# The gated layer's first product by seven products of halves, a batch at a time, in an attention and mixing kernel on one core

## The chip, the core and the metric

One core of one Trainium2 chip runs the whole program. The metric is device time in microseconds (us) from the first to the last instruction of an execution, and lower is better. The engines are named as in the profile: PE is TensorE (matmuls), PEld its weight loads, DVE is VectorE, ACT is ScalarE, POOL is GpSimd, SP is SyncE, which issues nearly all DMAs here.

## The reference, cut to what matters

Three layers follow each other. Attention over 4 batches x 8 heads, 576 positions and 64 values per head gives x of 4 x 576 x 512; a mixing layer adds a token mix and a channel mix; a gated layer ends it. The change touches the last one:

```
u  = x + (relu(x^T @ w_tok1) @ w_tok2)^T
x2 = u + relu(u @ w_ch1) @ w_ch2                 # 512 -> 1536 -> 512
h  = relu(x2 @ w_in)                             # 512 -> 1024
hp = h padded by one zero position at each end
conv_out = sum over t in 0..2 of conv_w[t] * hp[:, t:t+576, :]
out = (h * sigmoid(conv_out)) @ w_out            # 1024 -> 512
```

All data are 32-bit floats, and the layers' weights are 64-bit floats in memory.

## The kernel before, in words

Every large product runs in halves: a 32-bit operand is scaled by a power of two and split into a 16-bit high part (ScalarE) and a 16-bit low part (the rest; VectorE or GpSimd), and a product is three matmuls, high x high, high x low and low x high (`mm3`, L277 to L282). A column block of 128 outputs over 512 inputs and 288 positions is thus 4 x 3 = 12 matmuls of 128x128 weights and 288 columns.

Positions are cut into 8 chunks of 288 columns, two per batch (`CH`, `NCH`). The program has three stages that overlap. Attention with the token mix and an early part (5 of 12 blocks) of the channel mix runs until about 320 us. Then the rest of the channel mix (`channel_mix` with parts 1 and 2, 4 and 3 blocks), batch after batch, with `mix_input` and `mix_output` around it. Then the gated layer, chunk after chunk (`gated`, L1464).

No order is written by hand. Each step is a task (`T`, which is `Order.add`) with an engine, an assumed duration, a rank, what it reads and writes, and the PSUM buffers that it holds. `Order.run` (L60) plays them through: at each point it takes, on each engine, the task that can start first, and among those that could start at once the one of least rank. The instructions are then issued in that order, so each engine's order is fixed in the program; waits between engines follow from the data. Ranks of the matmuls are raised by `LATE` (1000) once or more, so that the matmuls of an earlier stage go first.

Weights come in blocks of 128x512 (`weight_set`): a DMA of 64-bit values into one of two staging tiles (`wraw`), an exponent step on ScalarE (L317), two joins on VectorE (L321, L322), a sum of squares (L517), then, once all blocks of a set are there and their common scale is known, the split into halves (L551 on ScalarE, L555 on VectorE). The halves of a block are written over the block before it. The slots are `WT[0..40]`: the first 15 (`NE`) lie in a pool that is open from the start, the next 10 (`NA`) in one that opens when attention's tiles are done, the others in one that opens on the left side when the token mix is done. `LATER` holds the ranks of the weights of the mixing parts 1 and 2.

The gated layer before, for each chunk c:

- The chunk of x2 is read back from memory (`chunk`, L598), its largest magnitude taken (L266) and spread to all partitions by a small 32-bit matmul with the identity (`spread`, L260), and the chunk is split (L591 ScalarE, L594 VectorE).
- For each of 8 column blocks m: `hf` is 12 matmuls into one of four PSUM banks ("w"). `relu` (L1508, ScalarE) moves the result to `hp_t[m]`. Then a 286 or 290 column wide gate: `conv0` (L1512, ScalarE), two taps (`conv`, L1518, VectorE), the sigmoid (L1522, ScalarE), the product (`mul`, L1526, VectorE), the high half (`gh`, L269, ScalarE) and the low half (`gl`, L275, GpSimd).
- For each of 4 output blocks d: `outp` is 24 matmuls over all 8 blocks into a "z" bank; `ocopy` (L1545, ScalarE) moves it out and `store` (L1549) issues a DMA.

Of the kernel before, what the change touches and what calls it, by code (L numbers as in the profile page):

```python
# [143 lines left out]
def fox_moe_kernel(  # L144
# [54 lines left out]
    NE = 15  # L199
    NA = 10  # L200
    NW = 41
# [10 lines left out]
    LATER = (-60.0, 0.0, 20.0)  # L212
    PER = 7.0

# [269 lines left out]
    def weight_set(name, blocks, raws, first, ranks, cranks, factor):  # L484

# [5 lines left out]
        bring = power_of if blocks[0][2][0].dtype == F32 else power_of_root  # L491
        if bring is power_of_root:
            factor *= 4.0
        for k, (kind, m, (src, dims)) in enumerate(blocks):
# [66 lines left out]

    us = {}
# [3 lines left out]
    PB = 2  # L566
    taken_res = [0]

    def parts(r):
        if r not in us:  # L570
            us[r] = [work.tile([128, KD, CH], F16, tag=n, name=n, bufs=2) for n in ("uh", "ul")]
        return us[r]
# [25 lines left out]
    def chunk(src, c, rank, reads, evac, scale, measure):  # L598

        r = chunks[0]  # L600
        chunks[0] += 1
        ku = ("u", counted["u"] % UB)
        counted["u"] += 1
        box = {}

        def load():
            box["u"] = pools["p2a"].tile([128, KD, CH], F32, tag="u", name="u", bufs=UB)
            nc.sync.dma_start(box["u"], src[:, :, c * CH:(c + 1) * CH].rearrange("k p s -> p k s"))

        def piece(k, lo):  # L610
            sl = slice(k, k + 2)
            divide(r, sl, lambda: box["u"][:, sl], scale)[lo]()

        T("SP", 0.4, rank - 6, load, reads=[*reads, ("p2a",)], writes=[ku], moved=2.4)
        measure(ku, box, rank + evac)
        for k in range(0, KD, 2):
            kh, kl = [[split_keys(r, x)[y] for x in (k, k + 1)] for y in range(2)]
            o = opening(r)
            rd = [ku, ("scale", id(scale))]
            T("ACT", 0.77, rank + evac, piece, k, 0, reads=[*rd, *o["reads"]], writes=kh + o.get("writes", []))  # L620
            T("DVE", 0.78, rank + evac, piece, k, 1, reads=[*rd, *kh], writes=kl)
        return r, [x for k in range(KD) for x in split_keys(r, k)]

    def channel_mix(c, part, rank, u_of, p_of, rts, tag, tag2, pe, evac):
# [6 lines left out]
        rpool, rbufs, rcount = rts  # L631
# [8 lines left out]
        def rh(m):  # L640
            t = pools[rpool].tile([128, 2, CH], F16, tag="r", name="r", bufs=rbufs)
            box["r", m] = t
            nc.scalar.activation(out=t[:, 0, :], in_=box["z", m], func=AF.Relu)  # L643

        def rl(m):
            t = box["r", m]
            nc.vector.scalar_tensor_tensor(t[:, 1, :], box["z", m], 0.0, f32(t[:, 0, :]), ALU.max, ALU.subtract)  # L647
# [21 lines left out]
        for k, m in enumerate(ms):  # L669
            kz = turn(tag)  # L670
            kr = ("r", rpool, rcount[0] % rbufs)
            rcount[0] += 1
            for j in range(KD):
                T("PE", MM * 3, rank + pe, m1, m, j, reads=[*ukeys, wkey("ch1", m)],
                  writes=[kz, kr, (*kr, "l")], ring=[kz])
            T("ACT", 0.4, rank + evac, rh, m, reads=[kz], writes=[kr], pools=[rpool], ring=[kz])
            T("DVE", 0.46, rank + evac, rl, m, reads=[kz, kr], writes=[(*kr, "l")], pools=[rpool], ring=[kz])
            rkeys += [kr, (*kr, "l")]
        for d in range(KD):
# [6 lines left out]
            for j, m in enumerate(ms):  # L686
                T("PE", MM * 3, rank + pe + 0.01, m2, d, m, pools=[rpool], ring=[kz],
                  writes=[kz, kd] if j == 0 and p_of is None else [kz],
                  reads=[wkey("ch2", x) for x in (ms if j == 0 else [m])] + rkeys + ([kd] if p_of and j == 0 else []))
            if p_of:  # L690
                T("DVE", 0.46, rank + evac, add, d, reads=[kz, back_key], writes=[kd], ring=[kz])
                continue
# [3 lines left out]
    def mix_input(c, rank):  # L696
# [9 lines left out]
        def load_half(x):  # L706
            if x == 0:
                us[r] = [pools["p2a"].tile([128, KD, CH], F16, tag=n, name=n, bufs=2) for n in ("vh", "vl")]
            nc.sync.dma_start(us[r][x], uhl_d[x, :, :, cols].rearrange("k p s -> p k s"))

        def load_u():
            box["u"] = pools["p2a"].tile([128, KD, CH], F32, tag="u", name="u", bufs=UB)
            nc.sync.dma_start(box["u"], u_d[:, :, cols].rearrange("k p s -> p k s"))

        def load_p():
            box["p"] = pools["p2a"].tile([128, KD, CH], F32, tag="p", name="p", bufs=PB)
# [15 lines left out]
    def mix_output(c, p_of, rank):  # L732
# [4 lines left out]
        T("SP", 0.4, rank, store, reads=[(p_of[1], d) for d in range(KD)], writes=[("x2_d", c)], moved=2.8)  # L737
# [5 lines left out]
    px = [power(f"px{c}") for c in range(NCH)]  # L743
    gs = const.tile([128, NCH, 3], F32, name="gs")
    um = [const.tile([128, GB], F32, name=f"um{b}") for b in range(B)]
    xm = [const.tile([128, 1], F32, name=f"xm{c}") for c in range(NCH)]

    with tc.manual_schedule():
# [3 lines left out]
        open_pool("r1")  # L752
        open_pool("we")
        for i in range(NE):
            WT[i] = pools["we"].tile([128, 512], F32, tag=f"w{i}", name=f"w{i}", bufs=1)
# [617 lines left out]
        rts1 = ("r1", 9, [0])  # L1373
# [16 lines left out]
        def turn_a2():  # L1390
            close_pool("a2")
            open_pool("p2a")
            late("p2a", range(NE, NE + NA))

        def turn_left():
# [8 lines left out]
            open_pool("p2b", 1, "left")  # L1404
            late("p2b", range(NE + NA, NW))
            open_pool("cp", 1, "left")
# [14 lines left out]
        at, first = at, at - 1  # L1421
# [11 lines left out]
        rts2 = ("p2a", 9, [0])  # L1433
# [143 lines left out]
        for c in range(NCH):  # L1577
            gated(c)
# [39 lines left out]
```

## Time and profile before

| | us |
|---|---|
| median of 3 runs | 717.15 |
| lowest and highest | 716.79, 717.42 |
| span of the profiled execution | 718.1 |
| TensorE busy in it | 698.7 |
| VectorE, ScalarE, GpSimd busy in it | 507.4, 428.5, 243.4 |

The rows of the trace are in a section below. A busy share is an average over stages with different limits. Matmuls are pipelined, so the mean duration of one (about 286 ns) is not what it costs; the count in a stretch of time tells that. Neighbouring operations of VectorE and ScalarE overlap by some 80 ns in the records, so the step from one start to the next is less than one's duration. The granted clock of 1.00 is the full 2.4 GHz of TensorE.

### The profile page before, as it was taken

What the parts mean: (1) busy time and instruction counts of PE and PEld (TensorE: products, weight loads), DVE (VectorE), ACT (ScalarE), POOL (GpSimd) and SP (SyncE); (2) the same over time, 40 slices, a digit from 0 to 9 for tenths busy, and PEclk for the clock granted to TensorE, in tenths of its full rate; (3) what the DMA queues carried; (4) which work ended last, traced back from release to release, by engine and by line L of the source; (5) the groups of instructions that cost most, each with busy time, mean ns of one, the idle gap of its engine ahead of it and who ended that gap; (6) DMA issues with size and microseconds to landing.
All of it is one profiled execution on the core that took longest, in us unless ns stands there. A gap on an engine that the chain in (4) does not pass through costs nothing.

```text
span 718.1 us, 16399 instructions
## 1 busy us (share of the span) xinstructions
PE 698.7 (97%) x6417; PEld 561.1 (78%) x6417; DVE 507.4 (71%) x1268; ACT 428.5 (60%) x940; POOL 243.4 (34%) x321
## 2 busy tenths in 40 slices
PE   6999888999999999999999999999999999999998
PEld 5889665878877788888888778778888778778786
DVE  6787878999987779537566857435778866875570
ACT  6987776586666544646574645112177766776671
POOL 2247562748453666240000212103023322322240
PEclk9999887999999999999999999999999999999999
DMA  9445769799995979785455765344211111100101
GB/s 225 141 127 189 193 175 235 120 258 226 248 239 138 199 122 223 189 282 150 144 172 147 250 221 161 99 133 144 66 56 58 51 59 34 51 27 25 34 17 50
DMA packets 153117, 101.98 MB, mean 142 GB/s; under 512 B 90000, under 2 KB 145168, under 8 KB 153040
## 3 DMA queue, kind: packets, MB, share of 16 engines
q1 hardware_dynamic: 152944, 100.79, 54.4%
q8 instruction: 50, 0.82, 0.5%
q14 instruction: 27, 0.22, 0.1%
q10 hardware_dynamic: 96, 0.15, 0.1%
HBM read 57.73 MB, written 23.59 MB: 113 GB/s over the span
## 4 chain that ended last, share of the span: by engine, by line
PE 87%; DVE 8%; ACT 1%; DMA 1%; SPq 1%; issue 1%; POOL 0%; DVEq 0%; ACTq 0%
PE w L280 15%; PE w L281 15%; PE w L282 15%; PE z L281 8%; PE z L282 8%; PE z L280 8%; PE z L994 6%; PE w L1083 3%; DVE pl L1033 2%; PE w L1051 2%; PE w L1235 2%; PE z L998 1%; PE w L260 1%; DVE ul L594 1%; PE w L1088 1%; PE w L1089 1%
## 5 line engine op out<-in xcount | busy, mean ns | idle before, releaser
L282 PEld LDWEIGHTS <-w 128*128 128x128 f16 x1280 | 125.6, 98 | 34.0 <-issue 1.9
L280 PEld LDWEIGHTS <-w 128*128 128x128 f16 x1280 | 125.3, 98 | 33.7 <-issue 2.4
L281 PEld LDWEIGHTS <-w 128*128 128x128 f16 x1280 | 125.3, 98 | 33.0 <-issue 1.7
L281 PE MATMUL w<-ul,w 128*128 128x288 f16 x416 | 120.0, 288 | 1.6 <-DVE ul L594 1.6
L280 PE MATMUL w<-uh,w 128*128 128x288 f16 x416 | 120.0, 289 | 1.3 <-ACT uh L591 1.1
L282 PE MATMUL w<-uh,w 128*128 128x288 f16 x416 | 119.9, 288 | 0.0
L275 POOL TENSOR_TENSOR g<-sg,g 128x286 f16<-128x286 f32 (+1 forms) x64 | 55.1, 867 | 150.8 <-ACT g L269 148.0
L1518 DVE SCALAR_TENSOR_TENSOR cv<-hp,cw,cv 128x286 f32<-128x286 f32 (+1 forms) x128 | 75.0, 593 | 38.3 <-ACT cv L1512 36.0
L1018 ACT ACTIVATE t<-t,m 128x192 f32<-128x192 f32 (+4 forms) x160 | 82.0, 551 | 18.1 <-DVE m L1012 14.9
L643 ACT ACTIVATE r<-w 128x288 f16<-128x288 f32 x96 | 39.3, 409 | 88.0 <-PE w L282 87.1
L1012 DVE CUSTOM_DVE_ANT_0 t<-z,mask 128x192 f32<-128x192 f32 (+4 forms) x160 | 70.3, 479 | 12.8 <-PE z L998 12.5
L720 POOL TENSOR_TENSOR p<-p,u 128x288 f32<-128x288 f32 x32 | 26.6, 863 | 149.7 <-DMA p<-p_d 115.1
L647 DVE SCALAR_TENSOR_TENSOR r<-w,r 128x288 f16<-128x288 f32 x96 | 43.3, 453 | 46.8 <-ACT r L643 46.2
L281 PE MATMUL z<-g,w 128*128 128x286 f16 (+1 forms) x256 | 73.3, 286 | 0.0
L280 PE MATMUL z<-g,w 128*128 128x286 f16 (+1 forms) x256 | 73.0, 285 | 0.0
L282 PE MATMUL z<-g,w 128*128 128x286 f16 (+1 forms) x256 | 72.9, 285 | 0.0
L280 PE MATMUL w<-vh,w 128*128 128x288 f16 x224 | 64.1, 286 | 0.0
L281 PE MATMUL w<-vl,w 128*128 128x288 f16 x224 | 64.1, 286 | 0.0
L282 PE MATMUL w<-vh,w 128*128 128x288 f16 x224 | 64.1, 286 | 0.0
L280 PE MATMUL z<-r,w 128*128 128x288 f16 x224 | 64.1, 286 | 0.0
L281 PE MATMUL z<-r,w 128*128 128x288 f16 x224 | 64.1, 286 | 0.0
L282 PE MATMUL z<-r,w 128*128 128x288 f16 x224 | 64.1, 286 | 0.0
(201 smaller groups left out, 1686.8 us busy)
## 6 DMA issues: line engine op xcount, KB each, us to landing
wraw<-in_moe_w_ch_dram SPq DMA_DIRECT2D x24, 512.0 KB, 4.2
qk<-in_qk_dram SPq DMA_DIRECT2D x15, 608.0 KB, 5.4
u_d<-us SPq DMA_DIRECT2D x8, 576.0 KB, 3.4
p_d<-res SPq DMA_DIRECT2D x32, 144.0 KB, 3.1
p<-p_d SPq DMA_DIRECT2D x8, 576.0 KB, 5.3
u<-u_d SPq DMA_DIRECT2D x8, 576.0 KB, 4.8
x_d<-p SPq DMA_DIRECT2D x8, 576.0 KB, 3.2
u<-x_d SPq DMA_DIRECT2D x8, 576.0 KB, 3.9
```

The lines of the kernel that those rows point to most:

```text
L275: nc.gpsimd.tensor_tensor(o, a, b, ALU.subtract)
L280: nc.tensor.matmul(ps, wh, xh, start=(first and i == 0), stop=False)
L281: nc.tensor.matmul(ps, wh, xl, start=False, stop=False)
L282: nc.tensor.matmul(ps, wl, xh, start=False, stop=(last and i == n - 1))
L643: nc.scalar.activation(out=t[:, 0, :], in_=box["z", m], func=AF.Relu)
L647: nc.vector.scalar_tensor_tensor(t[:, 1, :], box["z", m], 0.0, f32(t[:, 0, :]), ALU.max, ALU.subtract)
L720: nc.gpsimd.tensor_tensor(box["p"][:, d], box["p"][:, d], box["u"][:, d], ALU.add)
L994: nc.tensor.matmul(out_[x], t[r, Q0[i]:Q0[i] + 128], t[r, k0:k0 + n], start=first, stop=False)
L1012: nc.vector.tensor_tensor_reduce(to, z_t.pop((n, i)), mk, -0.125, 3e38, ALU.add, ALU.min, m_t[n][0:rows, i:i + 1])
L1018: nc.scalar.activation(out=tt[0:rows, o:o + w], in_=tt[0:rows, o:o + w], func=AF.Exp, bias=m_t[n][0:rows, i:i + 1], scale=-1.0)
L1083: nc.tensor.matmul(o[:, 0:65], p32(n)[:, 128 * blk:128 * blk + 128], vp32_t[g % 2][:, slot, hh, :], start=(j == 0), stop=(j == nb - 1))
L1518: nc.vector.scalar_tensor_tensor(cv, hp_t[m][:, s0 + t:s1 + t], cw[:, t, m:m + 1], cv, ALU.mult, ALU.add)
```

## The change

The weights of the first product, as a 2 x 2 matrix of halves (inputs 0 to 255 and 256 to 511; outputs 0 to 511 and 512 to 1023), and the inputs, as a 2 x 2 matrix of halves (inputs; the two chunks of a batch), are multiplied by seven products of halves in place of eight, with sums of the halves before and of the products after.

- `seven_set`: w_in's eight blocks stay in a staging area, four sums of halves (S1 to S4) are made in place on GpSimd, and seven matrices are split into 16-bit halves (`WO`), 1024 columns wide. w_out's blocks go into the same staging area afterwards.
- For each batch, four quarters of x2 are loaded, measured together and spread once; four sums (T1 to T4) are made on GpSimd, 576 columns wide, and seven split into halves, in one of two buffers.
- For each batch and each of four groups g: seven products of 6 matmuls each. The first two are copied out of PSUM by ScalarE, the five others are added to a former sum by VectorE on their way out, and two further sums are made on GpSimd. The results are both chunks of the column blocks g and g + 4. ReLU then runs in place over 576 columns, and the gate steps are 576 columns wide.
- `outp` takes the gates of a whole batch: for each d, both chunks into the two halves of one "z" buffer. In the last batch, the first two d take six of the eight blocks first and the last two later.
- The first batch's seven products get ranks among those of the last mixing batch.
- The tiles are laid out anew (one large tile is cut into several buffers; the gate's buffers lie over the mixing's), with 11 + 5 slots in the first pool. `LATER` is (-54.18, 42.07) for the mixing parts 1 and 2, where it was (-60, 0).

```diff
-    NE = 15
+    NK = 11
+    NE = 16
     NA = 10
-    NW = 41
+    NW = 35
+    NP = KF // 2
...
-    LATER = (-60.0, 0.0, 20.0)
+    LATER = (-54.18, 42.07, 88.75)
     PER = 7.0
+    INR = (40.21, -40.3, 85.43, 24.56)
+    OUTR = (123.16, -6.13, 204.2, 20.97)
+    XR, EV, EVP = -37.6, 17.72, 17.77
+    HFS = (12.58, 15.25, 57.25, 96.68)
+    HFP = (0.15, 8.3, 13.43, 20.78)
+    ORS = (23.83, 100.42, 126.06, 201.89)
+    OP = (14.95, 10.42, 3.66, 3.28)
...
+    WX = ("A11", "A12", "A22", "S1", "S3", "S2", "S4")
+    RX = ("B11", "B21", "B22", "T1", "T3", "T2", "T4")
+    PAIRS = {"A11": "B11", "S1": "T1", "S2": "T2", "S3": "T3", "A12": "B21", "A22": "T4", "S4": "B22"}
...
+        made = {"S1": ("a21", "a22", ALU.add), "S3": ("a11", "a21", ALU.subtract), "S2": ("a22", "a11", ALU.subtract),
+                "S4": ("a12", "a11", ALU.subtract)}
...
+        for n, x in enumerate(WX):
+            r = cat + cpace * n
+            if x in made:
+                a, b, _ = made[x]
+                T("POOL", 2.2, r - cpace, combine, x, reads=[sk[a], sk[b]], writes=[sk[at[x]]], pools=[tag])
+            T("ACT", 1.2, r, high, x, reads=[sk[at[x]], ("pw", name)], writes=[("wo", x, "h")], pools=[tag])
+            T("DVE", 1.5, r, low, x, reads=[sk[at[x]], ("pw", name), ("wo", x, "h")], writes=[("wo", x)], pools=[tag])
...
+        todo.event(nothing, after=["stin"], writes=[("W", i) for i in range(SB, NW)])
+        pout = late_set("out", [("out", m, row_block(w_out, m)) for m in range(KF)], list(range(SB + 1, SB + 1 + KF)), SB,
+                        T_2 + OUTR[0], OUTR[1], T_2 + OUTR[2], OUTR[3], 2.0 ** 13)
...
+        todo.event(turn_x, after=["r1"], writes=[("xfree",)])
+        todo.event(turn_f, after=[("part", EARLY)], writes=[("f", 1, x) for x in range(4)] + [("g", x) for x in range(G1)])
+        todo.event(turn_g, after=["mix"], writes=[("g", x) for x in range(G1, GB_N)])
...
+            T("PE", 0.55, pre, span, reads=[("xm", b, n) for n in range(4)], writes=[kw], ring=[kw])
+            T("DVE", 1.1, pre, lambda: power_of(px[b], box["ps"], 512), reads=[kw], writes=[sk], ring=[kw])
...
+            for x in RX:
+                if x in made:
+                    T("POOL", 1.3, pre, combine, x, reads=[uq(y) for y in made[x][1:]], writes=[uq(x)])
+                xo = ("xo", b % 2, x)
+                T("ACT", 0.77, pre, part, x, 0, reads=[uq(x), sk, ("xfree",)], writes=[xo])
+                T("DVE", 0.83, pre, part, x, 1, reads=[uq(x), sk, xo], writes=[(*xo, "l")])
...
+                mm3(ps, [(wh[:, sl[k]], wl[:, sl[k]], xh[:, k], xl[:, k]) for k in range(2)])
...
+            for g in range(NP):
...
+                at = (2 * LATE + T_2 + 6 * P2 if b == 0 else 3 * LATE + T_3) + HFS[b] + HFP[b] * g
+                ev = T_3 + HFS[b] + HFP[b] * g + EV
...
+                for x, o, i in (("A11", 0, None), ("S1", 1, None), ("S2", 2, 0), ("S3", 3, 2), ("A12", "11", 0),
+                                ("A22", "21", 3), ("S4", "12", 2)):
+                    kw = turn("w")
+                    T("PE", MM * 6, at, product, x, g, writes=[kw], ring=[kw],
+                      reads=[("wo", x), ("xo", b % 2, PAIRS[x]), ("xo", b % 2, PAIRS[x], "l"), *prev])
+                    prev = [kw]
+                    T("ACT" if i is None else "DVE", 0.42 if i is None else 0.52, ev, evac, x, g, f, o, i, ring=[kw],
+                      reads=[kw, *([] if i is None else [key(i)])], writes=[key(o)])
+                    if x == "S3":
+                        T("POOL", 0.88, ev, more_of, g, f, 2, 2, reads=[F[1]], writes=[F[2]])
+                        T("POOL", 0.88, ev, more_of, g, f, "22", 3, reads=[F[1], F[3]], writes=[hk["22"]])
+                for m in (g + NP, g):
...
+                    T("ACT", 0.77, ev + EVP, relu, m, reads=[("gs", b)], writes=h2)
...
+                    T("ACT", 0.8, ev + 2 * EVP, conv0, m, reads=[*h2, *[("cw", t) for t in range(3)]], writes=[kc])
+                    for t in (1, 2):
+                        T("DVE", 0.85, ev + 2 * EVP, conv, m, t, reads=[*h2, *[("cw", x) for x in range(3)]], writes=[kc])
+                    T("ACT", 0.75, ev + 3 * EVP, sig, m, reads=[kc], writes=[ks])
+                    T("DVE", 0.85, ev + 3 * EVP, mul, m, reads=[*h2, ("gs", b)], writes=[ks])
...
+                    T("ACT", 0.77, ev + 3 * EVP, gh, m, reads=[ks], writes=[kg])
+                    T("POOL", 1.3, ev + 3 * EVP, gl, m, reads=[ks, kg], writes=[(*kg, "l")])
...
+                for ks in (KS[0:6], KS[6:8]) if b == B - 1 and d < 2 else (KS,):
+                    for e in range(2):
+                        T("PE", MM * 3 * len(ks), 3 * LATE + at, outp, d, e, ks, ring=[kz],
+                          reads=[x for k in ks for x in gkeys[k]] + [wkey("out", k) for k in ks], writes=[(*kz, e)])
```

## Rows read from the trace of the kernel before

**Rows 1.** The page's first part: busy us, share of span, instructions, by engine.

```profile
PE 698.7 (97%) x6417; PEld 561.1 (78%) x6417; DVE 507.4 (71%) x1268; ACT 428.5 (60%) x940; POOL 243.4 (34%) x321
```

**Rows 2.** Stretches: length, busy us (instructions) of each engine; then clock, DMA share, GB/s.

```profile
0.00:20.00 20.00, 14.03 (x82) 10.68 (x82) 13.10 (x49) 13.40 (x30) 5.14 (x31) 0.91 0.93 240
...
80.00:100.00 20.00, 17.15 (x150) 13.31 (x151) 15.56 (x33) 13.63 (x25) 11.13 (x15) 0.83 0.70 168
100.00:120.00 20.00, 14.58 (x124) 9.46 (x120) 18.14 (x46) 13.49 (x28) 8.32 (x9) 0.83 1.04 232
...
500.00:520.00 20.00, 20.00 (x166) 16.00 (x164) 14.04 (x37) 4.06 (x9) 0.00 (x0) 1.00 0.22 60
...
560.00:580.00 20.00, 20.00 (x165) 15.83 (x164) 17.94 (x36) 15.17 (x36) 6.61 (x8) 1.00 0.15 47
```

**Rows 3.** Groups by shape, 380 to 720 us: count, busy us, mean ns, idle before.

```profile
L280 PE MATMUL w<-uh,w 128*128 128x288 f16 x256 | 73.2, 286 | 0.0
...
L1518 DVE SCALAR_TENSOR_TENSOR cv<-hp,cw,cv 128x286 f32<-128x286 f32 x64 | 38.1, 602 | 19.6 <-ACT cv L1512 18.4
L1518 DVE SCALAR_TENSOR_TENSOR cv<-hp,cw,cv 128x290 f32<-128x290 f32 x64 | 37.0, 584 | 18.7 <-ACT cv L1512 17.6
...
L1508 ACT ACTIVATE hp<-w,gs 128x288 f32<-128x288 f32 x64 | 31.3, 494 | 13.3 <-PE w L282 13.1
L659 DVE SCALAR_TENSOR_TENSOR p<-z,backs,p 128x288 f32<-128x288 f32 x60 | 30.9, 515 | 26.0 <-PE z L282 24.0 <-POOL p L720 1.9
L275 POOL TENSOR_TENSOR g<-sg,g 128x290 f16<-128x290 f32 x32 | 27.8, 875 | 59.7 <-ACT g L269 58.7 <-PE z L282 1.1
...
L647 DVE SCALAR_TENSOR_TENSOR r<-w,r 128x288 f16<-128x288 f32 x48 | 21.7, 453 | 24.0 <-ACT r L643 23.8
L1526 DVE SCALAR_TENSOR_TENSOR sg<-sg,gs,hp 128x286 f32<-128x286 f32 x32 | 20.6, 645 | 1.9 <-ACT sg L1522 1.4
...
L1526 DVE SCALAR_TENSOR_TENSOR sg<-sg,gs,hp 128x290 f32<-128x290 f32 x32 | 19.8, 628 | 2.5 <-ACT sg L1522 2.0
...
L266 DVE TENSOR_REDUCE xm<-u 128x1 f32<-128x1152 f32 x8 | 10.7, 1341 | 0.0
```

**Rows 4.** VectorE in order of time, 560 to 575 us: start, us, operation, count.

```profile
562.05 0.82 DVE L594 SCALAR_TENSOR_TENSOR ul<-u,px,uh 128x576 f16<-128x576 f32 x1 [0.48 <-ACT uh L591]
562.79 0.52 DVE L1526 SCALAR_TENSOR_TENSOR sg<-sg,gs,hp 128x290 f32<-128x290 f32 x1
563.22 1.07 DVE L1518 SCALAR_TENSOR_TENSOR cv<-hp,cw,cv 128x290 f32<-128x290 f32 x2
564.21 0.81 DVE L594 SCALAR_TENSOR_TENSOR ul<-u,px,uh 128x576 f16<-128x576 f32 x1
564.93 1.55 DVE L1518 SCALAR_TENSOR_TENSOR cv<-hp,cw,cv 128x286 f32<-128x286 f32 x2
566.39 1.17 DVE L1526 SCALAR_TENSOR_TENSOR sg<-sg,gs,hp 128x290 f32<-128x290 f32 x2
```

**Rows 5.** GpSimd in order of time, same stretch, same columns.

```profile
564.24 1.37 POOL L275 TENSOR_TENSOR g<-sg,g 128x290 f16<-128x290 f32 x1 [5.13 <-ACT g L269]
...
571.68 0.73 POOL L275 TENSOR_TENSOR g<-sg,g 128x286 f16<-128x286 f32 x1 [2.19 <-ACT g L269]
```

**Rows 6.** Groups by shape on GpSimd, whole span, columns as in rows 3.

```profile
L905 POOL TENSOR_TENSOR vp<-vf,vp 128x1024 f16<-128x1024 f32 x6 | 12.9, 2144 | 0.2
...
L275 POOL TENSOR_TENSOR w1l<-w,w1h 128x512 f16<-128x512 f32 x2 | 2.3, 1157 | 3.7 <-ACT w1h L269 3.7
```

**Rows 7.** The chain that ended last, in order of time: start, us, step, count.

```profile
319.28 0.44 PE w L260 x4
510.16 0.31 PE w L260 x2
714.76 0.50 ACT o L1545
```

More of the change, by code (lines that the diff above doesn't have):

```diff
@@ L482, in opened, with staged_set @@
         return [] if i < NE else [("p2a",)] if i < NE + NA else [("p2b",)]
-    def weight_set(name, blocks, raws, first, ranks, cranks, factor):
+    def staged_set(name, blocks, raws, ranks, crank, factor):
         nb = len(blocks)
@@ L490, in weight_set @@
         box = {}
[L491 removed]
+        bring = power_of if blocks[0][0].dtype == F32 else power_of_root
         if bring is power_of_root:
             factor *= 4.0
[L494 removed]
+        for k, (src, dims) in enumerate(blocks):
             i = raws[k]
@@ L596, in divide @@
         return hi, lo
[L598 to L622, printed above, removed]
+    lt = {}
     def channel_mix(c, part, rank, u_of, p_of, rts, tag, tag2, pe, evac):
@@ L1444, in fox_moe_kernel @@
                 mix_output(2 * b + e, ins[e][1], q + 3 * e)
-        pin = late_set("in", [("in", m, col_block(w_in, m)) for m in range(KF)], list(range(25, 33)), 24, T_2 + 60, 5.0,
-                       T_2 + 100, 3.0, 4.0)
+        nothing = lambda: None
+        SB = NE + NA
+        pin = seven_set("in", [col_block(w_in, m) for m in range(KF)], SB, [T_2 + INR[0] + INR[1] * k for k in range(KF)],
+                        T_2 + INR[2], INR[3], 2.0, "stin")
         for t in range(3):
@@ new lines, in turn_x, with turn_g, turn_f @@
+        def turn_x():
+            t = kept.bitcast(F16)
+            for i in range(2):
+                lt["x", i] = tiles_of(t[:, 28 * CH * i:28 * CH * (i + 1)], (2, 2, CH), 7)
+        def turn_g():
+            lt["g"].extend(tiles_of(lt["mix"].bitcast(F16), (2, S), GB_N - G1))
+        def turn_f():
+            lt["f"].append(tiles_of(more, (CH,), 4))
+            lt["g"] = tiles_of(more[:, 4 * CH:].bitcast(F16), (2, S), 2) + tiles_of(lt["second"].bitcast(F16), (2, S), G1 - 2)
+        GB_N, G1 = 12, 4
@@ new lines, in gl, with outp @@
+                pool_sub(gt[b, m][:, 1], lt["sg"][box["cv", m]], gt[b, m][:, 0])
+            KS = [m + x for m in range(NP) for x in (0, NP)]
+            def outp(d, e, ks):
+                sl, cs = slice(d * 128, (d + 1) * 128), slice(e * CH, (e + 1) * CH)
+                if e == 0 and KS[0] in ks:
+                    box["z", d] = bank("z")
+                ps = box["o", d, e] = box["z", d][:, e, 0:CH]
+                mm3(ps, [(halves("out", k)[0][:, sl], halves("out", k)[1][:, sl], gt[b, k][:, 0, cs], gt[b, k][:, 1, cs])
+                         for k in ks], KS[0] in ks, KS[-1] in ks)
@@ L1569, in gated @@
             for d in range(KD):
                 kz = turn("z")
[L1571 to L1578 removed]
+                at = T_3 + ORS[b] + OP[b] * d
@@ L1579, in fox_moe_kernel @@
+        for b in range(B):
+            gated(b)
         todo.run()
-        for name in ("cp", "p2b", "hp", "p2a", "we", "r1"):
+        for name in ("p2b", "hp", "p2a", "we"):
             close_pool(name)
```

303 lines of the change are left out of this document (180 added, 123 removed).

## The prediction

> **What bounds the kernel now.** I read the page's engine totals first, then the table by stretches of 20 us, then the groups by shape for the last 340 us, then the order of VectorE and GpSimd in one stretch. TensorE is busy for 698.7 us of 718.1 [rows 1]. The reader should not trust that share alone, but the count beside it: from about 300 us on, every 20 us holds 166 matmuls (165 in some), the gated layer's stretches among them [rows 2]. That is 20 / 166 = 0.1205 us for each 288-column matmul, with the granted clock at 1.00, which is the 2.4 GHz level. So the stage that the change touches is bound by the number of matmuls and by nothing else: VectorE has 14 to 18 us of work in 20 there, ScalarE up to 15, GpSimd up to 7 [rows 2]. TensorE's idle time lies elsewhere: 2.9 and 5.4 us at 80 to 120 us, where the clock also falls to 0.83, 6.0 us in the first 20 [rows 2], and the tail behind the last matmul, whose eviction begins at 714.76 [rows 7]. None of it is in the gated layer.
>
> **What is removed.** Before, the first product has 8 chunks x 8 column blocks x 4 x 3 = 768 matmuls; the three lines of the multiplication helper have 256 each [rows 3]. After: 4 batches x 7 products x 4 groups x 2 x 3 = 672. The second product stays at 768 (288 columns in place of 286 and 290). So 96 matmuls go: 96 x 0.1205 = 11.6 us, all on the path, as long as TensorE stays without a wait. That is the whole gain; nothing else in the change shortens TensorE's list.
>
> **What is added on TensorE.** The spread of the batch's maximum takes four columns once per batch in place of one column per chunk. One column took 0.31 us, two took 0.44 [rows 7]; at 0.13 for each further column (the records overlap) four take 0.7 to 0.9. I take 4 x 0.85 - 8 x 0.31 = 0.9 us.
>
> **What is added elsewhere, and its cover.** Work on the weights (four sums of 1024 columns on GpSimd, seven wider splits on ScalarE and VectorE in place of eight) lies in the mixing stage. There VectorE has some 6 us free in 20 even in the stretch that ends it [rows 2], and the weights are not wanted before its last batch: cost nothing. If that cover were gone, it is one sum (2.1 us by the 1024-column row [rows 6]) behind another. The second layer's weights now share the staging blocks and so come later, behind the last split of the first's; before, they were the same number of blocks in the same stage, so this too is covered, at a price of one block's chain if not. The inputs of batches 0 and 1 can be made there as well, since their halves have two buffers.
>
> The gate steps lie beside the matmuls, and VectorE is the one to add up. A 290-column product steps in 0.43 us (562.79 to 563.22), the two dependent taps in 0.99 (563.22 to 564.21), a 576-column split in 0.74 [rows 4]. So a 576-column step costs 0.3 more than a 290-column one: two taps 1.6, product 0.74. An addition from PSUM is not in the trace; its bounds are 0.37 and 0.515, from the split that reads PSUM (453 ns, less 80 ns of overlap) and the scaled addition in the mixing (515 ns) [rows 3]; I take 0.45, between them. One group (five additions, two gates): 5 x 0.45 + 2 x 2.34 = 6.9 us; 16 groups are 111 us (before: 64 x 1.42 = 91). The inputs of batches 2 and 3 are 4 maxima at half of 1341 ns [rows 3], seven splits of 0.74 and some 1.2 us of small steps: 9.1 each, 18 in all. The evictions of the mixing part that is left take 7. Together 136 us.
>
> For GpSimd, a 286-column subtraction alone took 0.73 us [rows 5], 512 columns 1.16 and 1024 columns 2.14 [rows 6], so 576 columns are 1.29. After: 32 x 1.29 (low halves of the gate), 32 x 0.73 (the two further sums per group) and 8 x 1.29 (input sums of two batches) = 75 us, against 64 x 0.87 = 56 before [rows 3].
>
> The two engines get in each other's way, and the trace shows it. The split at 564.21 and the subtraction at 564.24 overlap: the subtraction takes 1.37 us in place of 0.73 [rows 5], and the two taps behind it 1.55 in place of 1.07 [rows 4]. Over the stage, the taps took 602 and 584 ns on average and the products 645 and 628 [rows 3], against 0.52 alone [rows 4]: 64 x (0.082 + 0.064 + 0.117) = 17 us of waiting for 56 us of GpSimd work, 0.31 us for each. After: 75 x 0.31 = 23 us, so VectorE needs 136 + 23 = 159 us.
>
> It has this long: the matmuls from batch 0's first product (which goes in ahead of the last batch's second mixing part) to the point where the last batch's output needs its last two gates: (672 + 768 + 144) x 0.1205 = 191 us, less the 120 matmuls (14.5 us) behind that point, 176 us. So VectorE fits, with 17 us to spare, but at 90% over the whole window. The Trainium skill (SBUF — State Buffer, Who interferes with whom) says that a VectorE instruction with two SBUF inputs and a GpSimd one that reads SBUF lock a shared port pair for the whole instruction, and that additions with only one SBUF input do not contend. The trace agrees on the direction (1.37 against 0.73 us), but an average of 0.31 us per us of GpSimd work is less than full blocking. By the rule in full, VectorE would need 211 us; that is the second rival.
>
> ScalarE: the pass over PSUM (494 ns [rows 3]) becomes 32 copies of that size, ReLU becomes a pass of its own over 576 columns, and the three other passes are half as many and twice as wide. It has 15 of 20 us at most [rows 2] and stays about there: nothing on the path.
>
> One new coupling has a price. Before, a bank of the four was filled by 12 matmuls (1.45 us) and emptied by ScalarE; now by 6 (0.72 us), and in five of seven cases by VectorE. Three banks ahead give 2.2 us. If VectorE has just begun a 576-column step (0.82) behind a GpSimd subtraction (1.29) and then adds (0.5), that is 2.6: 0.4 to 1 us of TensorE wait. Bounds: nothing (no such wait before) to 8 us (16 groups, each hit for 0.5). I take one group in four, 2 us, near the lower end, since the stage before shows the same overlaps and no TensorE wait.
>
> **Sum**, against the profiled execution: 718.1 - 11.6 + 0.9 + 2.0 = 709.4 us. Its span is 0.9 above the median of the runs shown (717.15), so the forecast is 708.5 us; its own range, by the bounds of the waits, 706.5 to 714.5.
>
> **Rivals.**
> - Bank waits eat most of it: every group is hit once or more for 0.8 us or so, 13 us in all, 719.5 at worst and some 716 in the middle. For it: VectorE at 90% in strict order; against it: the matmuls of the second product, which need no VectorE, can stand between the groups.
> - Slower: VectorE becomes the bound, because of GpSimd. It decides from waits over 40 us (0.53 per us of GpSimd work, against 0.31 now); the gain is gone at 51 us (0.68); with full blocking, 75 us, the end is 35 us later. The middle of the losing part (63 us) gives 709.4 - 2.0 + 23 - 0.9 = 729.5; range 719 to 742. For it: single overlaps do cost a whole operation [rows 4, 5]; against it: the 80 additions and the maxima are a third of VectorE's list, and they read one SBUF input.
> - The later ranks shift the order of the first 160 us, where TensorE's idle time is [rows 2]. A third of the 8.3 us at 80 to 120 us saved, on top of the forecast without bank waits, is 704. Against it: the first part's ranks move by 6 units, and only the later part's by 42, whose work lies after 300 us.
> - The change gives TensorE fewer products but not earlier ones: it waits for weights or inputs of the first group, about as long as it saves: 717. Against it: the stage before has idle time on all others.
>
> **How the numbers follow.** A measurement of this kernel tells 0.2% (1.4 us) from no change. Forecast 0.63; bank waits 0.09; slower by VectorE 0.14; early order 0.07; late weights 0.07. Faster by over 0.2% (under 715.7): 0.63 + 0.07 + 0.05 + 0.02 = 0.77. Within 0.2%: 0.08, from the two middle rivals. Slower: 0.15. The range 705 to 717.5 leaves out the slower rival and about half of the early-order one.
>
> **What would show it.** Right: 672 matmuls for the first product, still 166 in 20 us up to the end, some waits of TensorE for additions of under 1 us each, VectorE at about 18 of 20 us. Wrong: TensorE waits that are long and stand in front of the second product (VectorE is the bound), or over 5 us in sum in front of the seven products (banks); taps of 576 columns with a mean well above 0.95 us (GpSimd blocks more than I count); a different idle time before 160 us (ranks).

## The result and the profile after

The changed kernel takes **726.34 us** (median of 4 runs, 723.21 to 726.61) against 717.28 us before (716.79 to 717.65): a ratio of 1.0114, interval 1.0094 to 1.0134. It is slower by 1.1%, where 708.5 us and faster was forecast; the range (705.0 to 717.5) does not hold it. The profiled execution of after has a span of 724.5 us and a time of 726.3, 1.8 more, as in most executions. By the same 1.8 the trace of before, with its span of 718.1, was an execution some 2.7 us above that kernel's median. A span of 715.4 stands for that median, and the differences below are taken from it.

The page's first part, after (columns as in [rows 1]):

```profile
PE 693.9 (96%) x6337; PEld 555.8 (77%) x6337; DVE 548.3 (76%) x1235; ACT 426.9 (59%) x855; POOL 305.9 (42%) x341
```

Groups by shape from 380 to 720 us, after; they answer [rows 3]:

```profile
L289 PE MATMUL w<-kept,wo 128*128 128x288 f16 x224 | 64.9, 290 | 3.2 <-ACT more L278 3.2
...
L1640 DVE SCALAR_TENSOR_TENSOR cv<-hp,cw,cv 128x576 f32<-128x576 f32 x64 | 62.8, 1005 | 3.3 <-ACT cv L1636 3.1
L1647 DVE SCALAR_TENSOR_TENSOR sg<-sg,gs,hp 128x576 f32<-128x576 f32 x32 | 33.3, 1055 | 1.1 <-ACT sg L1643 1.0
...
L1586 DVE SCALAR_TENSOR_TENSOR kept<-uh,px,kept 128x576 f16<-128x576 f32 x12 | 15.7, 1312 | 0.0
L607 DVE SCALAR_TENSOR_TENSOR wo<-stage,pw_in,wo 128x1024 f16<-128x1024 f32 x7 | 11.0, 1572 | 0.8 <-ACT wo L604 0.8
L1626 DVE TENSOR_TENSOR hp<-w,more 128x288 f32<-128x288 f32 x24 | 10.6, 454 | 10.9 <-PE w L291 9.9 <-POOL more L1629 1.0
...
L284 POOL TENSOR_TENSOR mix<-sg,mix 128x576 f16<-128x576 f32 x20 | 30.9, 1562 | 41.7 <-ACT mix L278 41.7
...
L601 POOL TENSOR_TENSOR stage<-stage 128x1024 f32<-128x1024 f32 x4 | 10.3, 2565 | 74.5 <-DVE wo L607 74.3
...
L1581 POOL TENSOR_TENSOR ul<-ul,ul 128x576 f32<-128x576 f32 x4 | 7.2, 1800 | 0.3
```

The removal is there: the first product's three lines have 224 matmuls each in place of 256. New on VectorE are the additions from PSUM (L1626); new on GpSimd are the four weight sums (L601) and sixteen input sums (L1581), four of each kind.

Stretches of 20 us, after (columns as in [rows 2]):

```profile
400.00:420.00 20.00, 17.03 (x124) 12.58 (x122) 17.21 (x20) 6.39 (x9) 17.59 (x12) 0.91 0.63 203
...
480.00:500.00 20.00, 17.75 (x132) 13.48 (x131) 13.58 (x23) 5.02 (x10) 5.55 (x6) 0.91 0.50 158
...
540.00:560.00 20.00, 18.34 (x149) 14.37 (x147) 19.71 (x29) 10.59 (x19) 6.52 (x5) 1.00 0.19 59
560.00:580.00 20.00, 20.00 (x166) 15.98 (x164) 17.93 (x33) 15.06 (x27) 14.04 (x13) 1.00 0.19 61
580.00:600.00 20.00, 20.00 (x167) 16.17 (x165) 19.96 (x25) 11.63 (x20) 10.34 (x7) 1.00 0.09 31
600.00:620.00 20.00, 17.84 (x133) 13.56 (x131) 19.13 (x27) 15.14 (x27) 15.37 (x11) 0.91 0.09 30
```

Before, each of these held 165 or 166 matmuls. Now 42 are missing at 400, 34 at 480, 17 at 540 and 33 at 600 us; with 13, 10 and 5 at 440, 640 and 680 us that is 154, and 154 x 0.1205 = 18.6 us. On the other side, by the starts in the traces, 96 matmuls are 11.7 us (0.122 each), of which the four wider spreads take back 1.7. So the path is 10.0 us shorter by TensorE's list and 18.6 us longer by holes in its work: 715.4 - 10.0 + 18.6 = 724.0, where the spans of after are 721.4 to 724.6. Note the 580 us stretch: VectorE busy for all 20 us, and TensorE loses nothing. What TensorE waited for, after (us in total, times, longest):

```profile
PE z L289 <- DVE mix L699: 5.6, 4, 2.2
PE w L289 <- ACT more L278: 3.2, 2, 2.2
PE z L290 <- DVE mix L687: 2.5, 3, 1.3
```

L699 and L687 are the evictions of the mixing stage (the steps that empty a PSUM buffer; the last L699 is at 561 us), not steps of the gated layer. From 380 us on neither of them ever waited for GpSimd. One hole in order of time: VectorE, then GpSimd, then TensorE (start, us, operation, count, idle time before it):

```profile
407.76 0.74 DVE L275 TENSOR_REDUCE xm<-uh 128x1 f32<-128x576 f32 x1
408.42 3.09 DVE L607 SCALAR_TENSOR_TENSOR wo<-stage,pw_in,wo 128x1024 f16<-128x1024 f32 x1
411.43 0.51 DVE L699 SCALAR_TENSOR_TENSOR mix<-z,backs,mix 128x288 f32<-128x288 f32 x1
...
404.08 4.03 POOL L760 TENSOR_TENSOR mix<-mix,u 128x288 f32<-128x288 f32 x4
408.08 5.63 POOL L601 TENSOR_TENSOR stage<-stage 128x1024 f32<-128x1024 f32 x2
...
411.99 0.28 PE L289 MATMUL z<-mix,more 128*128 128x288 f16 x1 [2.22 <-DVE mix L699]
```

GpSimd begins two weight sums at 408.08. VectorE's weight split begins 0.34 us later and takes 3.09 us; the shortest of the seven took 1.28. That is the first sum's 2.34 (the shortest of the four), less the 0.34, and then its own 1.28: 3.28, about the 3.09 seen. Behind the split in VectorE's queue stands the addition that empties the PSUM buffer TensorE wants next, and TensorE idles 2.22 us.

The hole at 484 us shows the same with an operation that has next to nothing to do. A product of two 128x1 tiles on VectorE took 1.35 us beside an input sum on GpSimd; the same line at 519 us, with GpSimd idle, took 0.15 us (columns as above):

```profile
481.27 1.79 POOL L1581 TENSOR_TENSOR ul<-ul,ul 128x576 f32<-128x576 f32 x1
481.73 1.35 DVE L1577 TENSOR_TENSOR gs<-gs,pw_out 128x1 f32<-128x1 f32 x1
519.15 0.15 DVE L1577 TENSOR_TENSOR gs<-gs,pw_out 128x1 f32<-128x1 f32 x1
```

It ended at 483.08, as the sum did (483.06). An input split of 0.81 us followed, then the addition L699, for which TensorE had waited 2.25 us.

A hole this long costs a second time. The place of the first hole in short stretches (columns as above):

```profile
408.00:412.00 4.00, 1.78 (x15) 1.28 (x14) 4.00 (x4) 1.15 (x1) 3.92 (x3) 1.00 0.82 251
412.00:413.00 1.00, 1.00 (x9) 0.80 (x9) 1.00 (x3) 0.00 (x0) 1.00 (x1) 1.00 0.99 275
413.00:417.00 4.00, 4.00 (x22) 2.61 (x20) 2.30 (x4) 1.15 (x1) 1.74 (x3) 0.57 0.55 190
```

After the hole, the 4 us row counts 22 matmuls where 33 would fit: the granted clock is 0.57 on average, most of the stretch at the 1.2 GHz level. The row also counts matmuls that lie across its edges, so the starts in the trace tell the cost better: for 3.3 us they follow each other at 0.24 us or a little less in place of 0.12, which is 1.7 us more. The three stretches at 0.91 are those with a hole of over 2 us, and behind each the loss is 1.7 us. By the starts, ten stops of TensorE cost 13.4 us and these three stretches 5.1, nearly all of the 18.6.

### The profile page after: what moved, and what is told of

It is laid out like the page before. It is cut to its first block, busy times and chain, and to the rows that moved or that the text cites. A ratio compares the mean times of both kernels' runs of the same rounds, so it can differ in the third digit from the quotient of the medians.

```text
span 724.5 us, 16138 instructions
## 1 busy us (share of the span) xinstructions
PE 693.9 (96%) x6337; PEld 555.8 (77%) x6337; DVE 548.3 (76%) x1235; ACT 426.9 (59%) x855; POOL 305.9 (42%) x341
## 5 line engine op out<-in xcount | busy, mean ns | idle before, releaser
L289 PE MATMUL w<-kept,wo 128*128 128x288 f16 x224 | 64.9, 290 | 3.2 <-ACT more L278 3.2
L284 POOL TENSOR_TENSOR xl<-xf,xh 128x320 f16<-128x320 f32 x32 | 30.2, 944 | 88.0 <-ACT xh L278 87.8
L1640 DVE SCALAR_TENSOR_TENSOR cv<-hp,cw,cv 128x576 f32<-128x576 f32 x64 | 62.8, 1005 | 3.3 <-ACT cv L1636 3.1
L290 PE MATMUL w<-kept,wo 128*128 128x288 f16 x224 | 64.9, 290 | 0.0
L291 PE MATMUL w<-kept,wo 128*128 128x288 f16 x224 | 64.8, 289 | 0.0
L1044 PE MATMUL z<-qk 64*128 64x288 f32 (+4 forms) x384 | 59.4, 427 | 1.6 <-DVE m L1062 1.6
L1077 POOL TENSOR_SCALAR ph<-t 128x1024 f16<-128x1024 f32 (+1 forms) x46 | 49.8, 1097 | 23.6 <-ACT t L1068 22.0
L1083 DVE SCALAR_TENSOR_TENSOR pl<-t,ph 128x1024 f16<-128x1024 f32 (+1 forms) x46 | 54.4, 1189 | 4.5 <-POOL ph L1077 2.9
L289 PE MATMUL w<-uh,kept 128*128 128x288 f16 x160 | 46.7, 292 | 1.9 <-ACT uh L655 1.1
L284 POOL TENSOR_TENSOR mix<-sg,mix 128x576 f16<-128x576 f32 x20 | 30.9, 1562 | 41.7 <-ACT mix L278 41.7
L290 PE MATMUL w<-ul,kept 128*128 128x288 f16 x160 | 46.8, 293 | 1.7 <-DVE ul L658 1.7
L291 PE MATMUL w<-uh,kept 128*128 128x288 f16 x160 | 46.9, 293 | 0.0
L290 PE MATMUL z<-mix,stage 128*128 128x288 f16 x160 | 45.8, 286 | 0.4 <-POOL mix L284 0.4
L289 PE MATMUL w<-kept 128*128 128x288 f16 x160 | 45.8, 286 | 0.0
L291 PE MATMUL w<-kept 128*128 128x288 f16 x160 | 45.8, 286 | 0.0
L290 PE MATMUL w<-kept 128*128 128x288 f16 x160 | 45.8, 286 | 0.0
L291 PE MATMUL z<-mix,stage 128*128 128x288 f16 x160 | 45.8, 286 | 0.0
L289 PE MATMUL z<-mix,stage 128*128 128x288 f16 x160 | 45.8, 286 | 0.0
L699 DVE SCALAR_TENSOR_TENSOR mix<-z,backs,mix 128x288 f32<-128x288 f32 x64 | 32.6, 513 | 16.0 <-PE z L291 15.2
```

The costliest lines, as they stand in the source:

```text
L284: nc.gpsimd.tensor_tensor(o, a, b, ALU.subtract)
L289: nc.tensor.matmul(ps, wh, xh, start=(first and i == 0), stop=False)
L290: nc.tensor.matmul(ps, wh, xl, start=False, stop=False)
L291: nc.tensor.matmul(ps, wl, xh, start=False, stop=(last and i == n - 1))
L699: nc.vector.scalar_tensor_tensor(t, box["o", d], back, t, ALU.mult, ALU.add)
L1044: nc.tensor.matmul(out_[x], t[r, Q0[i]:Q0[i] + 128], t[r, k0:k0 + n], start=first, stop=False)
```

## The experiments

**Theory A**: a GpSimd sum that reads two SBUF tensors holds up VectorE's two-input operations (those with both inputs in SBUF) until it ends; in the mixing stage the evictions queued behind them come late, and TensorE stops. **Rival B**: VectorE, with more work, is the bound; the sums on GpSimd help it. Later rivals: GpSimd's own queue, and the ranks (the places of the new steps in the order).

### The sums on VectorE, with everything else in place

```diff
-            nc.gpsimd.tensor_tensor(view(at[x]), view(a), view(b), op)
+            nc.vector.tensor_tensor(view(at[x]), view(a), view(b), op)
-                nc.gpsimd.tensor_tensor(o, p, q, ALU.subtract)
+                nc.vector.tensor_tensor(o, p, q, ALU.subtract)
```

> The changed kernel, with its 4 weight sums and 16 input sums on VectorE in place of GpSimd, each at the same point of the program; every other engine's order is the same. Theory A (a GpSimd sum locks VectorE out, and its late evictions stop TensorE, whose clock then falls): the waits of TensorE at 408 to 412, 445 to 447, 484, 548 and 613 us go, which cost 139 of the 154 matmuls missing from the 20 us rows after 380 us, 16.7 us; with some new delay by the sums themselves 710 to 714 us. Theory B (VectorE simply has too much to do, 19 to 20 of 20 us from 540 to 640): it gets 16 x 0.75 + 4 x 1.2 = 17 us more, and the time is 726 to 735 us.

Measured: **715.49 us**, ratio to before 0.9978 (0.9965 to 0.9991), 10.8 us less than the changed kernel, with the same order on TensorE. Stretches and groups of this run, columns as before:

```profile
400.00:420.00 20.00, 18.64 (x152) 14.59 (x150) 19.16 (x29) 8.89 (x16) 7.32 (x8) 1.00 0.59 182
...
480.00:500.00 20.00, 20.00 (x165) 15.98 (x164) 11.69 (x23) 3.64 (x8) 6.96 (x10) 1.00 0.67 208
...
L1586 DVE SCALAR_TENSOR_TENSOR kept<-uh,px,kept 128x576 f16<-128x576 f32 x12 | 10.2, 853 | 0.0
L607 DVE SCALAR_TENSOR_TENSOR wo<-stage,pw_in,wo 128x1024 f16<-128x1024 f32 x7 | 9.0, 1290 | 0.8 <-ACT wo L604 0.8
L601 DVE TENSOR_TENSOR stage<-stage 128x1024 f32<-128x1024 f32 x4 | 4.8, 1208 | 0.0
L1581 DVE TENSOR_TENSOR uh<-uh,uh 128x576 f32<-128x576 f32 x4 | 3.0, 746 | 0.0
```

VectorE has 4 x 1.21 + 16 x 0.75 = 17 us more to do, and the kernel is faster than the changed one: rival B falls. The splits shown are back from 1312 and 1572 ns to 853 and 1290, and no stretch in the window 380 to 700 us has a clock below 1.00. The time lies just over A's 710 to 714: 72 matmuls' time is still lost (8.7 us), and 715.4 - 10.0 + 8.7 = 714.1, where this run's span is 713.4.

### Each kind of sum by itself

Only the weight sums on VectorE, then only the input sums (one of the two edits above each):

> Only the 4 weight sums of 1024 columns on VectorE, the 16 input sums stay on GpSimd. Theory A: the 42 matmuls missing at 400 to 420 us come back, 5 us: 721 us, and the later waits stay. Theory B: nothing gained, since VectorE had free time there on average: 726 us or a little more.

> Only the 16 input sums of 576 columns on VectorE, the 4 weight sums stay on GpSimd. Theory A: the waits at 445, 484, 548 and 613 us go and the one at 408 to 412 stays: 714 to 718 us. Theory B: 12 us more for VectorE where it is full: 726 to 735 us.

Measured: weight sums 723.17 us (1.0072, 1.0051 to 1.0094), 3.2 us below the changed kernel; input sums 719.00 us (1.0027, 1.0008 to 1.0047), 7.3 below. 3.2 + 7.3 = 10.5 of the 10.8. The 3.2 us are little beside the scatter (720.95 to 723.85, against 723.21 to 726.61 for the changed kernel), but the traces show which holes went. With the weight sums on VectorE the hole of 2.2 us at 412 us shrinks to 0.4 and 1.0, and those beside the input sums stay (2.2 us at 482, 1.3 at 544, 2.2 at 610); with the input sums there it is the reverse (2.2 at 410, then none over 1.1). Both lie some 1 to 2 us over what A expected; B, 726 and above, holds for neither.

### The kernel before, with idle work for GpSimd

In the kernel before, beside each of the 16 weight splits of the gated layers GpSimd gets two 128x576 differences that nobody reads, or five memsets of the same tile:

```diff
+    def beside(t):
+        o, p, q = (hp_t[x][:, 1:S + 1] for x in (2, 0, 1))
+        pool_cast(o[:, 0:1], t[:, 0:1])
+        for _ in range(2):
+            nc.gpsimd.tensor_tensor(o, p, q, ALU.subtract)
...
+                    beside(WT[j])
```

With memsets, the last two lines are

```diff
+        for _ in range(5):
+            nc.gpsimd.memset(o, 0.0)
```

> The kernel before, with work added on GpSimd alone: behind each of the 16 splits of w_in's and w_out's blocks (395 to 453 us) GpSimd copies one column of the split, which only times it, and makes two differences of 128x576 floats from tiles that nothing else uses then (some 45 us in all). No result is changed and no other engine waits for them. Theory A (a GpSimd operation with SBUF inputs locks VectorE's two-input operations out): VectorE's splits behind them take 1.3 to 2 us in place of 0.75, TensorE waits for the mixing's additions, and the time goes up by 2 to 6 us. Rival (it was the chain of sum, split and product that came late, not the port): nothing waits for these sums, so the time stays within 0.2% of 717.

> The same, with five memsets of 128x576 in place of the two differences: GpSimd is as long at work at the same points (5 x 0.58 us), but reads nothing. Theory A: VectorE's operations keep their durations and the time stays within 0.2% of 717. Rival (any GpSimd work beside VectorE slows it, or the extra waits of the copies do): as slow as the run with differences.

Measured: 738.7 us (1.0296) with the differences, 736.4 (1.0269) with the memsets. By the times alone theory A misses both runs and the second run's rival is met: with memsets the kernel is about as slow. But as a measure of the time both failed: GpSimd also makes an addition that the mixing's eviction (L667) waits for, the idle work stood ahead of it, and from 380 us on VectorE waited 16.7 and 23.2 us for it. First differences, then memsets: what TensorE waited for, and groups from 380 to 480 us:

```profile
PE z L280 <- DVE p L667: 13.3, 5, 5.7
...
L488 POOL TENSOR_TENSOR hp<-hp,hp 128x576 f32<-128x576 f32 x32 | 48.3, 1511 | 2.6
L561 DVE SCALAR_TENSOR_TENSOR w<-w,pw_in,w 128x512 f16<-128x512 f32 x8 | 9.8, 1224 | 0.4 <-ACT w L557 0.4
L321 DVE TENSOR_SCALAR wraw<-wraw 128x512 int32<-128x512 int32 x10 | 7.8, 776 | 0.0
```

```profile
PE z L280 <- DVE p L667: 15.0, 3, 7.3
...
L488 POOL MEMSET hp<- 128x576 f32 x80 | 47.2, 590 | 4.6
L561 DVE SCALAR_TENSOR_TENSOR w<-w,pw_in,w 128x512 f16<-128x512 f32 x8 | 6.0, 756 | 0.4 <-ACT w L557 0.4
L321 DVE TENSOR_SCALAR wraw<-wraw 128x512 int32<-128x512 int32 x10 | 4.6, 459 | 0.0
```

The durations tell what the times can't. GpSimd was busy for as long in both (48.3 and 47.2 us), and VectorE's split of the first set's blocks took 1224 ns beside differences and 756 beside memsets (all 16 splits: 1140 and 758, and 809 in the kernel before). So it is not GpSimd's being busy that slows VectorE, but its reading of tensors. The Trainium skill (SBUF — State Buffer, Who interferes with whom) says that the port pair shared by the two engines is an exclusive lock, and that a VectorE instruction with two SBUF inputs contends with a GpSimd one that reads SBUF, not with one that only writes it. These two rows agree, and so does the 3.09 us split above.

### The changed kernel with memsets for the sums

```diff
-            nc.gpsimd.tensor_tensor(view(at[x]), view(a), view(b), op)
+            for _ in range(2):
+                nc.gpsimd.memset(view(at[x]), 0.01)
-                nc.gpsimd.tensor_tensor(o, p, q, ALU.subtract)
+                for _ in range(2):
+                    nc.gpsimd.memset(o, 0.01)
```

> The changed kernel in which each of the 4 weight sums and each of the 16 input sums on GpSimd is replaced by two memsets of the same tile, so these sums are left out of what is computed; GpSimd stays busy for about as long and nothing else moves. In the runs on the kernel before, 32 GpSimd differences of 128x576 (1411 ns median) beside the weight splits raised VectorE's 128x512 two-input split from 742 ns to a mean of 1140 ns, while 80 memsets with the same total of GpSimd time (47 against 48 us) left it at 758 ns. Theory A (the cost of the change is that a GpSimd operation with two inputs holds up VectorE's two-input operations, and evictions behind them come late): with memsets the hold-up is gone although GpSimd is as busy, so the time is that of the sums on VectorE or a little less: 711 to 716 us. Rival B (the cost is GpSimd's own queue: its sums stand ahead of other work, or their results come late): the time stays at 722 to 727 us.

Measured: **710.65 us**, ratio 0.9898 (0.9879 to 0.9918). Groups of this run:

```profile
L1588 DVE SCALAR_TENSOR_TENSOR kept<-uh,px,kept 128x576 f16<-128x576 f32 x12 | 10.3, 858 | 2.3 <-ACT kept L1590 2.2
...
L602 POOL MEMSET stage<- 128x1024 f32 x8 | 7.5, 956 | 74.5 <-DVE wo L608 74.3
L1583 POOL MEMSET ul<- 128x576 f32 x16 | 9.2, 588 | 1.7 <-DVE kept L1588 1.2
```

The memsets stand in the same places of GpSimd's queue, in all 26 us against the sums' 37 (16 x 1.66 + 4 x 2.57), and 15.7 us are gone. No wait for L699 or L687 is left in the mixing stage. The time is a little under A's 711 to 716; the rival of GpSimd's queue (722 to 727) falls, though the 11 us less on GpSimd are not told apart from the missing reads here.

### Shorter sums

```diff
-            nc.gpsimd.tensor_tensor(view(at[x]), view(a), view(b), op)
+            for m in range(NP):
+                nc.gpsimd.tensor_tensor(view(at[x])[:, m], view(a)[:, m], view(b)[:, m], op)
-                nc.gpsimd.tensor_tensor(o, p, q, ALU.subtract)
+                for k in range(2):
+                    nc.gpsimd.tensor_tensor(o[:, k], p[:, k], q[:, k], ALU.subtract)
```

> The changed kernel in which each of the 4 weight sums on GpSimd is cut into one operation for each of its blocks of 256 columns, and each of the 16 input sums into two operations of 288 columns; the same work in the same order and in all a little longer (GpSimd's 128x288 additions take 0.79 us, so 1.58 us for two against 1.40 us for one). In the changed kernel VectorE's two-input operations beside a GpSimd sum take up to the length of the sum longer (the 128x576 split 0.80 us alone, 1.96 us at most beside a sum of 1.40). Theory A1 (VectorE is held up until the end of the one GpSimd operation, and then goes ahead): in pieces a hold-up lasts at most 0.8 us and fewer evictions come late, 716 to 721 us. Theory A2 (VectorE is held up as long as GpSimd has such operations waiting in its queue): the hold-ups stay as long as they were, 722 to 727 us.

Measured: 720.75 us, ratio 1.0047 (1.0030 to 1.0063), 5.6 below the changed kernel. Groups and TensorE's waits of this run:

```profile
L608 DVE SCALAR_TENSOR_TENSOR wo<-stage,pw_in,wo 128x1024 f16<-128x1024 f32 x7 | 9.2, 1309 | 6.7 <-ACT wo L605 6.7
...
L1583 POOL TENSOR_TENSOR uh<-ul,uh 128x288 f32<-128x288 f32 x8 | 9.8, 1241 | 0.0
...
PE w L289 <- ACT more L278: 4.8, 2, 3.8
PE z L289 <- DVE mix L700: 2.7, 4, 0.9
```

A1, as expected: the same reads in the same order in shorter instructions cost less. The longest weight split fell from 3.09 to 1.38 us, and the longest wait for the mixing's addition (L699, here L700) from 2.2 to 0.9; one wait of 1.5 for its other eviction is left. The sums as a whole became longer (the 32 pieces of 288 columns took 1.10 us on average where 0.79 is the shortest, 35 us in all against 27 for the 16 whole sums). So late results are not the main cause: the sums took longer, and the time fell. The wait for ScalarE, whose input split needs the last sum, grew from 2.2 to 3.8. So cutting is half a cure.

### Other ranks, with the sums on VectorE, on GpSimd, and with more on VectorE

```diff
-    LATER = (-54.18, 42.07, 88.75)
+    LATER = (-68.42, 33.31, 76.79)
...
-                T("POOL", 2.2, r - cpace, combine, x, reads=[sk[a], sk[b]], writes=[sk[at[x]]], pools=[tag])
+                T("DVE", 1.25, r - cpace, combine, x, reads=[sk[a], sk[b]], writes=[sk[at[x]]], pools=[tag])
...
-                    T("POOL", 1.3, pre, combine, x, reads=[uq(y) for y in made[x][1:]], writes=[uq(x)])
+                    T("DVE", 0.75, pre, combine, x, reads=[uq(y) for y in made[x][1:]], writes=[uq(x)])
```

Beside these edits the first kernel has those of the first experiment. The other tuples of ranks (INR, OUTR, XR, EV, EVP, HFS, HFP, ORS, OP) get other values too. The second kernel keeps the sums on GpSimd and has ranks alone; the third also puts the gate's 32 second additions (L1629) on VectorE, with ranks of its own.

> The changed kernel with the sums on VectorE, entered as VectorE's work of 1.25 and 0.75 us in the order that is planned, and with other ranks for the additions, the weight steps and the input steps, so that the splits and sums stand elsewhere between the evictions. With the sums on VectorE and the old ranks, 72 matmuls' time (8.7 us) were still idle, most of it before the additions of the mixing stage. Theory A (late evictions are what is left, and where the splits stand decides how many there are): some of the 8.7 us come back, 708 to 714 us. Rival B (what is left does not hang on the ranks): 714.5 to 717 us. Rival C (the ranks of the change were the best order for it): 717 to 725 us.

> The changed kernel with its sums on GpSimd as they are, and other ranks alone. Theory A (each sum with two inputs holds VectorE up for its length wherever it stands): ranks can move the 20 sums but not remove them, so the time stays above that of the sums on VectorE: 717 to 725 us. Rival B (the place that the ranks of the change gave to the sums is at fault): 711 to 716 us, as good as the sums on VectorE. Rival C (the ranks are without effect): 723 to 727 us.

> The changed kernel with the sums on VectorE and also the 32 second additions of the gate (128x288, two inputs, 0.80 to 1.43 us each on GpSimd), planned as VectorE's work, with ranks of its own. On VectorE each takes about 0.52 us by the 128x288 additions of the mixing, 17 us in all. Theory A (GpSimd's two-input operations cost more than the same work on VectorE): 706 to 714 us. Rival B (VectorE, now with some 33 us more than in the kernel before, becomes the bound in the gated layer): 716 to 730 us.

Measured: **711.81 us** (0.9912, 0.9890 to 0.9934) with the sums on VectorE; 718.79 (1.0017, 0.9998 to 1.0036) with them on GpSimd; 717.63 (0.9998, 0.9982 to 1.0014) with the second additions on VectorE too. Stretches of the first, and TensorE's waits in the second:

```profile
400.00:420.00 20.00, 19.83 (x162) 15.57 (x160) 19.68 (x30) 9.53 (x16) 10.42 (x8) 1.00 0.52 173
...
480.00:500.00 20.00, 20.00 (x165) 15.97 (x164) 13.75 (x28) 6.67 (x12) 7.58 (x10) 1.00 0.56 178
...
600.00:620.00 20.00, 19.85 (x162) 15.66 (x161) 19.31 (x32) 15.15 (x26) 14.24 (x12) 1.00 0.00 1
```

```profile
PE z L289 <- DVE mix L699: 3.0, 6, 0.9
PE w L289 <- DVE f L1626: 2.0, 2, 1.2
```

The first two came out as theory A expected. The first beats both kernels. Ranks alone are worth 7.5 us, so the places of the sums are part of the fault and not only the engine; but with the sums on GpSimd their holes only become shorter (none over 1.2 us; two of 1.2 and 0.9 us close together at 567 and 569 us still cost the clock, 0.91 in that stretch), and no gain over before is left. Ranks and engine don't add up: 14.5 us together, 10.8 and 7.5 alone. The third kernel has two changes at once (the additions and its ranks): TensorE there waited for GpSimd's low halves of the gate (1.6 and 1.1 us at most) and for additions (2.2 us in sum). It lies in rival B's range and missed theory A's; it shows no gain, and whether the additions, VectorE's load or the ranks are to blame stays open.

## Why the prediction was wrong

- **What is removed**: right. 672 matmuls for the first product, and the 11.6 us are 11.7 by the starts (a 20 us row also counts matmuls that lie across its edges, so 20 / 166 is a little low).
- **What is added on TensorE**: 0.9 us forecast, 1.7 measured. A spread of four columns held TensorE for 0.89 us, four times; a spread of one column for 0.22 in seven of eight cases, and the 0.31 that the forecast took for all was the longest. The net saving is 10.0 us, and with the holes it gives the spans of after and of the kernel with its sums on VectorE to within 1 us.
- **Weights and inputs in the mixing stage, "cost nothing"**: this step failed. The cover named was VectorE's 6 us free in 20 and a late due time of the weights. Neither was what mattered. Six free us are an average; TensorE needs each eviction soon after its last matmul, and an eviction stands behind whatever split VectorE has begun. The prediction priced a lost cover at one sum of 2.1 us for GpSimd's own chain, and did not ask what a sum does to the split beside it and the eviction behind that, though it used that very hold-up for the gated stage. Its own row had it: a subtraction took 1.37 in place of 0.73 beside a split [rows 5]. Measured, the sums cost 10.8 us by the engine they are on (3.2 and 7.3 by kind), and 15.7 against the kernel with memsets in their places, where TensorE has no wait left in the mixing stage.
- **The hold-up's size**: right as an average, though the taps' mean of 1.005 us is above the 0.95 that was named as a sign. In the changed kernel from 380 us on, the taps, products, input and weight splits took 64 x 0.20 + 32 x 0.25 + 28 x 0.40 + 7 x 0.29 = 34 us more than their shortest records, beside 118 us of GpSimd's two-input work (L284, L1629, L1581, L601): 0.29 us for each, where 0.31 was forecast. It does its harm by single hold-ups of 1 to 2 us in front of an eviction, which a mean doesn't show.
- **VectorE's load**: the stage came out heavier, 19.2 us of 20 busy on average from 540 to 640 us where 18 was forecast. That is not the bound: at 580 us it was busy for 19.96 and TensorE had 167 matmuls. The rival in which VectorE becomes the bound because of GpSimd has the right pair of engines, and by luck a range (719 to 742) that holds the time, but the wrong place and mechanism: a lack of capacity in the gated stage, where the loss is lateness, more than half of it in the mixing stage.
- **Bank waits in front of the seven products**, 2.0 us: 3.2 were seen, with a loss of clock behind the longer one. The cause was not an addition on VectorE. ScalarE, for which the prediction wrote "nothing on the path", should have copied the first bank out. In the longer wait (2.2 us) it stood behind an input split that waited for the last input sum (GpSimd, 1.80 us for each of the last three), in the shorter behind a sigmoid that waited for the taps.
- **The price of one operation**: an addition was put at a step of 0.45; it lasts 0.452, but the step from one start to the next is 0.37, so 80 of them take 6 us less than forecast. Sums of 576 columns 1.29 against 1.40 at the shortest, of 1024 columns 2.14 against 2.34; the further sums of the gate 0.73 against 0.79. The largest of these errors was on the safe side, and VectorE's load was not the bound.
- **The clock**: not in the sum at all. Each of the three holes over 2 us is followed by matmuls at the 1.2 GHz level, 1.7 us each.
- **Later ranks**: the rival looked for them in the first 160 us, where TensorE was idle for 15.1 us before and 14.3 after. Where another set of ranks made a difference (7.5 us with the sums on GpSimd), the holes that went lie after 400 us.

Open is how much of the 8.7 us that were left with the sums on VectorE belongs to GpSimd's other two-input work in the gated stage (the taps there still took 992 ns on average where 0.81 is common); the best kernel still loses 3.9 us to stops in its traced execution, the fastest of its four, and its median is 1.4 us more.

## What to carry to other kernels

Cover is a matter of lateness and not of busy share: for each step that is moved beside a stage that TensorE bounds, find the eviction that stands behind it in its engine's queue, and add the longest hold-up that step can have there. Elementwise sums of two SBUF tensors that are moved to GpSimd "for free" hold up VectorE's operations on two SBUF tensors until they end; here they ran in half the time on VectorE itself (0.75 against 1.40 us), and the kernel gained by giving it more work. If such work has to stay on GpSimd, cut it short and put it where no eviction is due.

## What the runs showed of the hardware

- The additions that read PSUM and one SBUF tensor took 443 to 460 ns in the changed kernel, however busy GpSimd was (454 on average in the row above). A reduction of one input that lay wholly beside a weight sum, at 412.22, took 0.74 us, as the one at 407.76.
- One-input operations are not all safe: the 128x512 integer steps of the weight loading took 776 ns beside differences and 459 beside memsets (438 in the kernel before).
- The hold-up goes both ways and by whole instructions: two weight sums beside the 3.09 us split took 5.63 us, where two of 2.34 are 4.7; the second, which began while the split ran, took 3.21.
